# Linear attention feeding a GELU MLP on one core: block-diagonal states from chunk 4 on, outputs beside the next scores, and an opening with more idle matmuls

## The chip, the cores and the metric

The kernel runs on one core of a Trainium2 chip. The metric is the device time of one execution in microseconds (us). Before the change the median of eight runs is 226.21 us, with 225.3 the fastest and 226.98 the slowest. One execution was also taken with the hardware profiler: it took 225.3 us, and the span of its instructions is 223.3 us, so that 2.0 us lie around the span.

## What is computed

Two stages follow each other. The first is decayed linear attention over blocks, for 4 sequences of 768 positions, 8 heads and 64 channels a head. The second is an MLP with exact GELU over the 3072 tokens, 512 to 2048 to 512.

```
for b in range(nb):                      # block = 64
    intra = (q_b @ k_b.T * Dmask) @ v_b
    inter = (q_b * lam_pow) @ kv_state
    out_b = intra + inter
    kv_state = lam**block * kv_state + (k_b * rev_pow).T @ v_b
...
x = out.transpose(0, 2, 1, 3).reshape(B * S, H * D)
h = x @ w_in
out = gelu(h) @ w_out
```

## The kernel before

The kernel takes the sequence in chunks of 128 positions, six to a sequence and 24 in all. Four chunks make a group of 512 tokens, and there are six groups. While TensorE does the MLP of group g, it also does the attention of the four chunks that make group g+1, in short stretches between the MLP's blocks of four matmuls. The opening does chunks 0 to 3 by themselves, with nothing to put beside them but idle matmuls on zeros (L321) that keep TensorE busy. The MLP of the last group has no attention beside it.

A chunk has these steps. `load` brings k, q and v by DMAs that POOL issues. `decay_k` scales k by a power of the decay. The transposes of k and q come either from TensorE (`transposes`, chunks 0 to 7) or from SP's transposing DMAs (`dma_transposes`, chunks 8 to 23), the latter after POOL has scaled q to `q_hat`. `scores` makes eight products, each with 64 rows of the array (L189), and VectorE (DVE) masks them (L193). `next_state` makes the new state: eight products with 64 columns of the array (L202), then DVE adds the decayed old state, and POOL (or ACT in the opening) decays the sum for the next chunk (L212, L214). `outputs` adds eight products of 64 rows by 64 columns with the state (L223) and eight with 64 columns for the masked scores (L227), and the result is cast into `x_t` (by ACT in the opening, L231, by DVE later, L233).

The MLP of a group is 16 blocks `mm1` (L245, four matmuls of 512 columns, then a GELU on ACT) and 16 blocks `mm2` (L257, likewise four, and a copy and a store after every fourth block of an output row).

What sets the order: every engine runs its instructions in program order. For groups 1 to 5 the list `todo` gives each chunk's steps a place as a fraction of the group's MLP, and the loop at the end puts a step before the first block that is not earlier than its place. Scores with the new state stand at one place and the outputs of the same chunk about half a chunk later, so each chunk breaks into the MLP twice. Loads are issued by `prefetch`, called at the step `begin`. PSUM has eight banks: two each for the tags `sc`, `mh` and `mo`, one each for `o` and `t`. The pool `work` has three buffers for each tag, so `k_dec` of a chunk can be written once the state product of the chunk three before it has read its own.

Of the kernel before, what the change touches and what calls it, by code (L numbers as in the profile page):

```python
# [8 lines left out]
F32 = mybir.dt.float32  # L9
BF16 = mybir.dt.bfloat16  # L10
# [5 lines left out]
def kernel(  # L16
# [24 lines left out]
    NG = NCH // M  # L41
    assert NG * M == NCH

# [103 lines left out]
    def decay_k(c, eng):  # L147

        if c.sb == NB - 1:
            return  # L150
        c.k_dec = work_pool.tile([128, H, D], BF16, tag="kd", name="k_dec")
        if eng is nc.scalar:
            for h in range(H):
                nc.scalar.activation(c.k_dec[:, h, :], c.k[:, h, :], ACT.Copy, scale=lam_k[:, h:h + 1])
        else:
            eng.tensor_mul(c.k_dec, c.k, lam_k[:, :, None].to_broadcast((128, H, D)))  # L156

    def transposes(c):
        if c.early:

            t_ps = [bank([128, HP, C], BF16, tag, "t_ps") for tag in ("mh", "mo")]
        else:
# [6 lines left out]
        c.qT = work_pool.tile([128, HP, C], BF16, tag="qT", name="qT")  # L169
        if c.early and c.n > 0:  # L170
            nc.scalar.copy(c.kT, t_ps[0])
        else:
            nc.vector.tensor_copy(c.kT, t_ps[0])  # L173
# [21 lines left out]
    def next_state(c):  # L195
        if c.sb == NB - 1:
            return
        kv_ps = bank([128, HP, D], F32, "t", "kv_ps")
        for hp in range(HP):
            for hi in range(2):  # L200
                h = 2 * hp + hi
                nc.tensor.matmul(kv_ps[hi * D:(hi + 1) * D, hp, :], c.k_dec[:, h, :], c.v[:, h, :],  # L202
                                 start=True, stop=True)
        new = work_pool.tile([128, HP, D], BF16, tag="state", name="state")
        if c.sb == 0:
# [3 lines left out]
        old = work_pool.tile([128, HP, D], F32, tag="old", name="old")  # L209
        if c.early:  # L210
            for hp in range(HP):
                nc.scalar.activation(old[:, hp, :], new[:, hp, :], ACT.Copy, scale=lam_c[:, hp:hp + 1])  # L212
        elif c.sb < NB - 2:
            nc.gpsimd.tensor_mul(old, new, lam_c_b)  # L214
        states[c.n + 1] = new, old

    def outputs(c, x_t, off):
        o_ps = bank([128, HP, C], F32, "o", "o_ps")
        if c.sb > 0:
            for hp in range(HP):  # L220
# [8 lines left out]
        x_o = x_t[:, :, off * C:(off + 1) * C]  # L229
        if c.early:  # L230
            nc.scalar.copy(x_o, o_ps)  # L231
        else:
            nc.vector.tensor_copy(x_o, o_ps)  # L233
# [75 lines left out]
    nc.scalar.activation(warm, pos, ACT.Gelu)  # L309

    def early(s):
# [4 lines left out]
    idle_ps = bank([128, 512], F32, "o", "idle_ps")  # L316

    def keep_warm(n):

        for _ in range(n):  # L320
            nc.tensor.matmul(idle_ps, idle[:, :128], idle, start=True, stop=True)  # L321

# [6 lines left out]
    keep_warm(2)  # L329
    next_state(live[0])  # L330
    outputs(live[0], xT[0], 0)
# [12 lines left out]
    for s in range(1, NS):  # L344
# [3 lines left out]


    total = NK2 * 4 * M * C + M * NK2 * 512  # L350
    todo = []
    for n in range(M, NCH):
        g, i = n // M - 1, n % M
        first, end = (0.66, 1.0) if g == 0 else (0.0, 0.97)
        at = lambda f: (g + first + (end - first) * (i + f) / M) * total
# [4 lines left out]
    def step(kind, n):  # L360
        g = n // M - 1
        if kind == 0:
            live[n] = begin(n)
            if g > 0:
                dma_transposes(live[n])
            decay_k(live[n], nc.gpsimd)
            prefetch(n + 4)
        elif kind == 1:
            if g == 0:
                transposes(live[n])  # L370
        elif kind == 2:
# [4 lines left out]

    prefetch(2 * M - 1)
    done = 0
    for g in range(NG):
        if g + 1 < NG:  # L380
            alloc_x(g + 1)
        for run, cost in mlp_blocks(g):
            while todo and todo[0][0] <= done:
# [36 lines left out]
```

## Time and profile before

| what | value |
|---|---|
| median of eight runs | 226.21 us (225.3 to 226.98) |
| profiled execution, its span | 225.3 us, 223.3 us |
| TensorE matmul busy | 213.7 us of the span |
| DVE, ACT, POOL busy | 61.4, 89.2, 111.6 us |
| chain that ended last | 78% TensorE |

The eight runs are 225.3, 226.67, 226.98, 225.91, 226.5, 226.78, 225.4 and 225.73 us. The profile's page gives each engine's busy time and the chain of work that ended last. Its views go further: the timeline lists the instructions in order of time with the idle time before each and what ended it, and the view by stretches sums the busy time of each engine between two times and gives the clock that TensorE was granted there, 1.00 being full. A matmul's own duration includes its way through the array, so the pace of a run of matmuls is read from one start to the next.

### The profile page before, as it was taken

To read this page: it belongs to the slowest core of one execution; us is meant where nothing else is said; L and a number is where in the kernel's file an instruction comes from. 1 tells how busy PE (TensorE), PEld (TensorE's weight loads), DVE (VectorE), ACT (ScalarE), POOL (GpSimd) and SP (SyncE) were. 2 spreads that over 40 slices of the span, in tenths; PEclk is the share of its full clock that TensorE was granted. 3 is DMA by queue.
4 is the path that set the end of the run, shared out by engine and by line. 5 is a ranking of instruction groups with operands and counts; after the bars stand their busy time and mean duration, and the time that the engine had idled before them with its cause. 6 is when DMAs were issued, how large, how long until landed. Compare 5 with 4: busy or idle time off the path is not lost.

```text
span 223.3 us, 3859 instructions
## 1 busy us (share of the span) xinstructions
PE 213.7 (96%) x1571; PEld 102.2 (46%) x1571; DVE 61.4 (27%) x109; ACT 89.2 (40%) x173; POOL 111.6 (50%) x132
## 2 busy tenths in 40 slices
PE   7886999899899999999999999999999999999993
PEld 2354444455444444444444444444444444444452
DVE  3575000267542142142142142142142142100000
ACT  6895665110356412255312356311346311467121
POOL 8998333899999994054855991043141000000000
PEclk9995899999999999999999999999999999999998
DMA  6999999999999999759679999013331111200112
GB/s 41 144 162 183 195 206 182 154 205 151 146 153 155 148 127 148 138 90 112 55 89 131 175 149 158 1 50 103 109 74 23 23 50 68 74 0 3 47 47 94
DMA packets 100273, 24.37 MB, mean 109 GB/s; under 512 B 92960, under 2 KB 97312, under 8 KB 100256
## 3 DMA queue, kind: packets, MB, share of 16 engines
q0 software_dynamic: 79104, 13.64, 85.3%
q1 hardware_dynamic: 21152, 10.50, 21.5%
q8 instruction: 12, 0.20, 0.4%
q14 instruction: 5, 0.04, 0.1%
HBM read 27.27 MB, written 6.29 MB: 150 GB/s over the span
## 4 chain that ended last, share of the span: by engine, by line
PE 78%; DMA 10%; POOL 9%; issue 1%; DVE 0%; ACT 0%; POOLq 0%
PE o_ps L257 34%; PE h_ps L245 32%; DMA w_out_t<-in_moe_w_out_dram 8%; PE o_ps L227 3%; PE sc_ps L189 3%; PE o_ps L223 3%; DMA k_t<-in_k_dram 2%; POOL q_t L65 2%; POOL v_t L65 2%; PE kv_ps L202 2%; POOL k_t L65 2%; PE o_ps L272 2%; POOL w_in_t L87 1%; POOL w_out_t L91 1%; POOL k_dec L156 1%
## 5 line engine op out<-in xcount | busy, mean ns | idle before, releaser
L245 PE MATMUL h_ps<-x_t,w_in_t 128*128 128x512 bf16 x384 | 87.6, 383 | 1.2 <-DVE x_t L233 0.8
L257 PE MATMUL o_ps<-w_out_t,g_t 128*128 128x512 bf16 x368 | 84.6, 380 | 0.0
L247 ACT ACTIVATE g_t<-h_ps 128x512 bf16<-128x512 f32 x96 | 57.3, 597 | 38.9 <-PE h_ps L245 38.9
L245 PEld LDWEIGHTS <-w_in_t 128*128 128x128 bf16 x384 | 36.5, 98 | 44.3 <-issue 2.6
L257 PEld LDWEIGHTS <-g_t 128*128 128x128 bf16 x368 | 34.0, 98 | 39.5
L193 DVE TENSOR_TENSOR sc_m<-sc_ps,dmask 128x512 bf16<-128x512 f32 x48 | 30.9, 686 | 65.7 <-PE sc_ps L189 65.5
L262 ACT COPY o_sb<-o_ps 128x512 f32<-128x512 f32 x23 | 13.5, 586 | 84.3 <-PE o_ps L257 81.0
L214 POOL TENSOR_TENSOR old<-state,lam_c 128x256 f32<-128x256 bf16 x12 | 7.4, 618 | 48.4 <-DVE state L208 25.1
L65 POOL DMA_DIRECT2D k_t<-in_k_dram x24 | 22.1, 922 | 3.7 <-DMA w_out_t<-in_moe_w_out_dram 1.7
L65 POOL DMA_DIRECT2D q_t<-in_q_dram x24 | 21.5, 895 | 4.9 <-DMA w_out_t<-in_moe_w_out_dram 3.3
L233 DVE CAST x_t<-o_ps 128x512 bf16<-128x512 f32 x20 | 13.8, 690 | 35.6 <-PE o_ps L227 35.6
L65 POOL DMA_DIRECT2D v_t<-in_v_dram x24 | 21.3, 889 | 3.9 <-DMA w_in_t<-in_moe_w_in_dram 1.7
L156 POOL TENSOR_TENSOR k_dec<-k_t,lam_k 128x512 bf16<-128x512 bf16 x18 | 19.0, 1053 | 0.5 <-DMA k_t<-in_k_dram 0.4
L181 POOL TENSOR_TENSOR q_hat<-q_t,lam_p 128x512 bf16<-128x512 bf16 x16 | 16.8, 1047 | 0.0
L227 PE MATMUL o_ps<-sc_m,v_t 128*64 128x128 bf16 x192 | 10.6, 232 | 0.0
L189 PEld LDWEIGHTS <-kT 64*128 64x128 bf16 x192 | 5.7, 97 | 9.9 <-issue 8.0
L189 PE MATMUL sc_ps<-qT,kT 64*128 64x128 bf16 x192 | 10.0, 226 | 0.2 <-DVE qT L174 0.2
L223 PE MATMUL o_ps<-qT,state 64*64 64x128 bf16 x160 | 8.7, 230 | 1.3 <-ACT x_t L231 1.3
L223 PEld LDWEIGHTS <-state 64*64 64x64 bf16 x160 | 5.5, 110 | 8.1 <-issue 7.8
L321 PE MATMUL idle_ps<-idle 128*128 128x512 bf16 x19 | 8.0, 579 | 1.2 <-DVE idle L94 1.2
L173 DVE COPY kT<-t_ps 128x512 bf16<-128x512 bf16 x5 | 2.1, 422 | 22.3 <-PE t_ps L167 22.2
L227 PEld LDWEIGHTS <-v_t 128*64 128x64 bf16 x192 | 6.4, 113 | 3.1 <-issue 1.4
(42 smaller groups left out, 75.4 us busy)
## 6 DMA issues: line engine op xcount, KB each, us to landing
out_dram<-o_sb SPq DMA_DIRECT2D x23, 256.0 KB, 2.5
k_t<-in_k_dram POOLq DMA_DIRECT2D x24, 128.0 KB, 5.0
q_t<-in_q_dram POOLq DMA_DIRECT2D x24, 128.0 KB, 5.2
v_t<-in_v_dram POOLq DMA_DIRECT2D x24, 128.0 KB, 5.8
w_in_t<-in_moe_w_in_dram POOLq DMA_DIRECT2D x4, 512.0 KB, 8.7
w_out_t<-in_moe_w_out_dram POOLq DMA_DIRECT2D x4, 512.0 KB, 15.5
kT<-k_t SPq DMA_TRANSPOSE x16, 4.9
qT<-q_hat SPq DMA_TRANSPOSE x16, 4.1
```

Of the source, the lines that this page charges most:

```text
L65: nc.gpsimd.dma_start(raw[n, name], chunk_of(name, n))
L156: eng.tensor_mul(c.k_dec, c.k, lam_k[:, :, None].to_broadcast((128, H, D)))
L181: nc.gpsimd.tensor_mul(q_hat, c.q, lam_p[:, :, None].to_broadcast((128, H, D)))
L189: nc.tensor.matmul(sc_ps[hi][:, hp, :], c.kT[p, hp, :], c.qT[p, hp, :], start=True, stop=True)
L193: nc.vector.tensor_mul(c.sc_m[:, :, hi, :], sc_ps[hi], dmask_r[:, :, hi, :])
L223: nc.tensor.matmul(o_ps[p, hp, :], states[c.n][0][p, hp, :], c.qT[p, hp, :], start=(hp == 0), stop=False, skip_group_check=True)
L227: nc.tensor.matmul(o_ps[hi * D:(hi + 1) * D, hp, :], c.v[:, 2 * hp + hi, :], c.sc_m[:, hp, hi, :], start=(c.sb == 0 and hp == 0), stop=Tru ...
L233: nc.vector.tensor_copy(x_o, o_ps)
L245: nc.tensor.matmul(h_ps, w_in_t[:, ki, kf * 128:(kf + 1) * 128], x_t[:, ki, :], start=(ki == 0), stop=(ki == NK1 - 1))
L247: nc.scalar.activation(g_t[:, kf, :], h_ps, ACT.Gelu)
L257: nc.tensor.matmul(om[io], g_t[:, kf, io * C:(io + 1) * C], w_out_t[:, kf, :], start=(kf == 0), stop=(kf == NK2 - 1))
L262: nc.scalar.copy(o_sb, om[io])
```

## The change

From chunk 4 on, the state is kept as a full 128 by 128 block for each pair of heads, with zeros off the diagonal blocks: four products of 128x128 make it, and four products use it, in place of eight and eight on parts of the array. The new DVE steps multiply by `lam_blk`, which holds the decay on the diagonal blocks and zero elsewhere; the decay on POOL is gone. Chunk 3 writes its state into the zeroed `first_blk`. The scale of k from chunk 4 on is `lam_m`. In groups 1 to 5 the outputs of a chunk are put at the same place as the scores of the next. Beside group 0's MLP the steps of chunks 4 to 7 stand in a table written by hand, `group0`, by the number of the block. POOL's loads and scalings for chunks 4 to 9 are written out. In the opening the decay of k for chunk 1 moves from ACT to DVE, chunk 2's scores move ahead of chunk 1's outputs, chunk 3's state product moves into group 0's MLP, and nine idle matmuls are added (28 against 19).

```diff
+    lam_blk = consts.tile([128, HP, 128], F32)
+    first_blk = consts.tile([128, HP, 128], BF16)
+    nc.vector.memset(lam_blk, 0.0)
+    nc.vector.memset(first_blk, 0.0)
...
+    def make_lam_blk():
+        for hi in range(2):
+            p = slice(hi * D, (hi + 1) * D)
+            nc.vector.tensor_copy(lam_blk[p, :, p], lam_c_b[p])
...
-            eng.tensor_mul(c.k_dec, c.k, lam_k[:, :, None].to_broadcast((128, H, D)))
+            scale = lam_k if c.early else lam_m
+            eng.tensor_mul(c.k_dec, c.k, scale[:, :, None].to_broadcast((128, H, D)))
...
-            both = bank([128, 2, HP, C], BF16, "t", "t_ps")
-            t_ps = [both[:, 0], both[:, 1]]
+        t_ps = [bank([128, HP, C], BF16, tag, "t_ps") for tag in ("mh", "mo" if c.early else "mh")]
...
-        if c.early and c.n > 0:
+        if c.n > 0:
             nc.scalar.copy(c.kT, t_ps[0])
...
+        if not c.early:
+            return next_state_full(c)
...
+        if c.n == M - 1:
+            for hi in range(2):
+                p = slice(hi * D, (hi + 1) * D)
+                nc.vector.tensor_add(first_blk[p, :, p], kv_ps[p], states[c.n][1][p])
+            states[c.n + 1] = first_blk, None
+            return
...
+    def next_state_full(c):
+
+        kv_ps = bank([128, HP, 128], F32, "t", "kv_ps")
+        for hp in range(HP):
+            nc.tensor.matmul(kv_ps[:, hp, :], c.k_dec[:, 2 * hp:2 * hp + 2, :], c.v[:, 2 * hp:2 * hp + 2, :],
+                             start=True, stop=True)
+        new = work_pool.tile([128, HP, 128], BF16, tag="state_f", name="state")
+        if c.sb == 0:
+            nc.vector.tensor_mul(new, kv_ps, lam_blk)
+        else:
+            tmp = work_pool.tile([128, HP, 128], F32, tag="tmp", name="tmp")
+            nc.vector.tensor_add(tmp, kv_ps, states[c.n][0])
+            nc.vector.tensor_mul(new, tmp, lam_blk)
+        states[c.n + 1] = new, None
+
+    def outputs(c, x_t, off):
+        o_ps = bank([128, HP, C], F32, "mh" if c.n == M - 1 else "o", "o_ps")
+        if c.sb > 0 and not c.early:
             for hp in range(HP):
...
-        elif c.sb < NB - 2:
-            nc.gpsimd.tensor_mul(old, new, lam_c_b)
...
+                nc.tensor.matmul(o_ps[:, hp, :], states[c.n][0][:, hp, :], c.qT[:, hp, :],
+                                 start=(hp == 0), stop=False, skip_group_check=True)
...
-        if c.early:
+        if c.n < 2 * M:
             nc.scalar.copy(x_o, o_ps)
...
+        if s == 1:
+            decay_k(live[s], nc.vector)
         transposes(live[s])
-        decay_k(live[s], nc.scalar if s < 2 else nc.gpsimd)
...
+    keep_warm(1)
     early(2)
     next_state(live[1])
+    scores(live[2])
+    decay_state(live[1])
+    outputs(live[1], xT[0], 1)
+    keep_warm(1)
     early(3)
-    outputs(live[1], xT[0], 1)
-    scores(live[2])
     next_state(live[2])
     outputs(live[2], xT[0], 2)
     scores(live[3])
+    keep_warm(5)
     outputs(live[3], xT[0], 3)
-    next_state(live[3])
+    decay_state(live[2])
+    make_lam_blk()
+    keep_warm(2)
...
+    for n, name in [(4, "k"), (4, "q"), (4, "v"), (5, "k"), (5, "q"), (5, "v"), (6, "k"), (6, "q")]:
+        load(n, name)
+    begin_decayed(4)
+    for n, name in [(6, "v"), (7, "k"), (7, "q"), (7, "v"), (8, "k")]:
+        load(n, name)
+    live[5] = begin(5)
+    begin_decayed(6)
+    for n, name in [(8, "q"), (8, "v")]:
+        load(n, name)
+    begin_decayed(7)
+    next_load[0] = 9
+    prefetch(9)
...
+    group0 = {
+        1: [lambda: next_state(live[3])],
+        22: [lambda: transposes(live[4])],
+        24: [lambda: scores(live[4])],
+        25: [lambda: transposes(live[5]), lambda: next_state(live[4]), lambda: x1(4)],
+        26: [lambda: scores(live[5])],
+        27: [lambda: transposes(live[6])],
+        28: [lambda: x1(5), lambda: scores(live[6])],
+        29: [lambda: transposes(live[7]), lambda: next_state(live[6])],
+        30: [lambda: x1(6), lambda: scores(live[7])],
+        31: [lambda: next_state(live[7]), lambda: x1(7)],
+    }
...
-        fs = (-0.5, 0.0, 0.5, 1.05) if g == 0 else (-0.45 if n == 2 * M else -1.0, 0.0, 0.35, 0.75)
-        todo += [(at(f), kind, n) for kind, f in enumerate(fs)]
+        at = 0.06 + 0.245 * i
+        fs = [at - (0.18 if n == 2 * M else 0.32), None, at, at + 0.245 if i < M - 1 else 0.965]
+        todo += [(round((g + f) * total), -kind, n) for kind, f in enumerate(fs) if f is not None]
...
-            prefetch(n + 4)
+            prefetch(n + 3)
```

TensorE, end of the opening: what follows chunk 3's scores (`sc_ps`). Before, the products with the state and with the masked scores, then chunk 3's own state product (`kv_ps`), then the MLP (`h_ps`):

```order
L189 MATMUL sc_ps_379<-qT,kT 128x128
...
L223 MATMUL o_ps<-qT,state 64x128
...
L227 MATMUL o_ps<-sc_m,v_t 64x128
...
L202 MATMUL kv_ps<-v_t,k_dec 64x64
...
L245 MATMUL h_ps<-x_t,w_in_t 128x512
```

The same place now:

```order
L196 MATMUL sc_ps_379<-qT,kT 128x128
...
L349 MATMUL idle_ps<-idle 128x512
...
L257 MATMUL o_ps<-qT,state 64x128
...
L261 MATMUL o_ps<-sc_m,v_t 64x128
...
L349 MATMUL idle_ps<-idle 128x512
...
L279 MATMUL h_ps<-x_t,w_in_t 128x512
...
L211 MATMUL kv_ps<-v_t,k_dec 64x64
```

Five idle matmuls stand between scores and outputs and two behind the outputs, and the state product has moved behind the MLP's first block.

TensorE, group 1, one chunk's part of the MLP before: scores and state product (`kv_ps`) at one place, the state's and scores' outputs at another, 12 MLP matmuls between them:

```order
L245 MATMUL h_ps<-x_t,w_in_t 128x512
...
L189 MATMUL sc_ps_1024<-qT,kT 128x128
...
L202 MATMUL kv_ps<-v_t,k_dec 64x64
...
L245 MATMUL h_ps<-x_t,w_in_t 128x512
...
L223 MATMUL o_ps<-qT,state 64x128
...
L227 MATMUL o_ps<-sc_m,v_t 64x128
...
L245 MATMUL h_ps<-x_t,w_in_t 128x512
```

And now, where chunk 8's outputs and chunk 9's scores meet:

```order
L279 MATMUL h_ps<-x_t,w_in_t 128x512
...
L251 MATMUL o_ps<-qT,state 128x128
...
L261 MATMUL o_ps<-sc_m,v_t 64x128
...
L196 MATMUL sc_ps_993<-qT,kT 128x128
...
L236 MATMUL kv_ps<-v_t,k_dec 128x128
...
L279 MATMUL h_ps<-x_t,w_in_t 128x512
```

One stretch has taken the place of two; the products with full 128x128 blocks (L251 and L236, four each) stand at its two ends.

POOL, from the loads of chunk 6 to the scaling of chunk 8's q. Before, the scaling of chunk 4's k (`k_dec`) came after chunk 7's loads; one piece of the difference:

```order
 L65 DMA q_t<-in_q_dram 128x8x64 [waits DMASW3_49]
-L65 DMA v_t<-in_v_dram 128x8x64 [waits DMASW4_49]
+L167 TENSOR_TENSOR k_dec<-k_t,lam_m 128x512 [waits DMASW4_49,DVE_49,PE_49]
+L65 DMA v_t<-in_v_dram 128x8x64
 L65 DMA k_t<-in_k_dram 128x8x64 [waits DMASW5_49]
 L65 DMA q_t<-in_q_dram 128x8x64 [waits DMASW6_49]
 L65 DMA v_t<-in_v_dram 128x8x64 [waits DMASW7_49]
-L156 TENSOR_TENSOR k_dec<-k_t,lam_k 128x512 [waits PE_49,Activation_49]
 L65 DMA k_t<-in_k_dram 128x8x64 [waits DMASW0_49]
+L167 TENSOR_TENSOR k_dec<-k_t,lam_m 128x512 [waits DMASW2_49,PE_49,Pool_49]
+L65 DMA q_t<-in_q_dram 128x8x64 [waits DMASW1_49]
```

The scalings of chunks 4 and 6 have moved ahead among the loads, and chunk 8's `q_hat` is the seventh instruction behind chunk 6's scaling: behind chunk 9's loads and ahead of chunk 10's.

More of the change, by code (lines that the diff above doesn't have):

```diff
@@ L41 @@
     NG = NCH // M
-    assert NG * M == NCH
+    assert NG * M == NCH and M == 4 and NB == 6
     ctx.enter_context(tc.manual_schedule())
@@ L309, with keep_warm @@
     nc.scalar.activation(warm, pos, ACT.Gelu)
+    def keep_warm(n):
+        idle_ps = bank([128, 512], F32, "mo", "idle_ps")
+        for _ in range(n):
+            nc.tensor.matmul(idle_ps, idle[:, :128], idle, start=True, stop=True)
     def early(s):
         live[s] = begin(s, early=True)
+        if s == 1:
+            decay_k(live[s], nc.vector)
         transposes(live[s])
-        decay_k(live[s], nc.scalar if s < 2 else nc.gpsimd)
[L316 to L321, printed above, removed]
+        if s != 1:
+            decay_k(live[s], nc.scalar if s == 0 else nc.gpsimd)
     keep_warm(9)
@@ L330 @@
     next_state(live[0])
+    decay_state(live[0])
     outputs(live[0], xT[0], 0)
@@ L381 @@
             alloc_x(g + 1)
-        for run, cost in mlp_blocks(g):
+        for i, (run, cost) in enumerate(mlp_blocks(g)):
+            if g == 0:
+                for act in group0.get(i, []):
+                    act()
             while todo and todo[0][0] <= done:
```

33 lines of the change are left out of this document (14 added, 19 removed).

## The prediction

> **What bounds the kernel now.** I read the page first, for the whole span.
>
> ```profile
> span 223.3 us, 3859 instructions
> PEclk9995899999999999999999999999999999999998
> PE 78%; DMA 10%; POOL 9%; issue 1%; DVE 0%; ACT 0%; POOLq 0%
> ```
>
> TensorE is most of the chain that ended last; the DMA and POOL shares lie in the opening. The granted clock falls in the fourth and fifth of 40 slices. So I cut the span into the opening, group 0 (first MLP matmul to group 1's first) and the rest; two answers of the view by stretches:
>
> ```profile
> 17.10:20.55 3.45, 2.57 (x33) 1.78 (x33) 2.27 (x5) 1.89 (x6) 3.45 (x6) 0.51 1.16 170
> 20.55:23.96 3.41, 2.93 (x21) 1.48 (x20) 0.45 (x2) 1.82 (x6) 1.79 (x3) 0.50 1.24 206
> 23.96:37.00 13.04, 13.04 (x62) 5.96 (x61) 0.00 (x0) 8.88 (x16) 4.38 (x5) 1.00 1.29 199
> ```
>
> ```profile
> 21.89:59.41 37.52, 36.05 (x273) 17.58 (x273) 12.77 (x24) 12.97 (x24) 25.69 (x29) 0.97 1.97 180
> 59.41:92.68 33.27, 33.27 (x249) 15.38 (x249) 8.91 (x15) 11.31 (x19) 26.93 (x31) 1.00 1.84 148
> ```
>
> Group 1 is TensorE from end to end (33.27 of 33.27 us). From 17.1 to 23.96 the clock is half. What one chunk costs TensorE is read from starts in the timeline, beside the pace of undisturbed MLP matmuls in the chain (13.81/64 = 0.216 us each):
>
> ```profile
> 192.21 13.81 PE h_ps L245 x64
> ```
>
> ```profile
> 59.41 2.75 PE L245 MATMUL h_ps<-x_t,w_in_t 128*128 128x512 bf16 x12 [0.79 <-DVE x_t L233]
> 62.09 0.40 PE L189 MATMUL sc_ps<-qT,kT 64*128 64x128 bf16 x8
> 62.41 0.32 PE L202 MATMUL kv_ps<-v_t,k_dec 128*64 128x64 bf16 x8
> 62.66 2.76 PE L245 MATMUL h_ps<-x_t,w_in_t 128*128 128x512 bf16 x12
> 65.36 0.41 PE L223 MATMUL o_ps<-qT,state 64*64 64x128 bf16 x8
> 65.70 0.41 PE L227 MATMUL o_ps<-sc_m,v_t 128*64 128x128 bf16 x8
> 66.05 4.49 PE L245 MATMUL h_ps<-x_t,w_in_t 128*128 128x512 bf16 x20
> ...
> 52.73 1.90 PE L257 MATMUL o_ps<-w_out_t,g_t 128*128 128x512 bf16 x8
> 54.47 0.39 PE L167 MATMUL t_ps<-ident,k_t 128*128 128x128 bf16 x4
> 54.69 0.39 PE L167 MATMUL t_ps<-ident,q_t 128*128 128x128 bf16 x4
> 55.01 0.41 PE L227 MATMUL o_ps<-sc_m,v_t 128*64 128x128 bf16 x8
> ```
>
> Twelve MLP matmuls should take 2.59; they take 2.68 before scores and 2.70 before outputs. Transposes, which use the whole array, start 1.74 after eight MLP matmuls, as 8 x 0.216 asks, and four of them take 0.22 (0.055 each); from the last four to the half-array product it is 0.32. So a **turn** from whole-array products to a part costs about 0.10. I take the same 0.10 for a turn between two kinds of parts, and for one back to the whole, where it sits inside the 0.32, 0.25, 0.34 and 0.35 us of the four sets above.
>
> The Trainium skill has a rule for it ("TensorEngine Tiling (Array Packing)", Key Properties): changing the tiling mode drains the engine. The rows agree, at 0.10 us.
>
> **Groups 1 to 5, part by part.** A chunk costs now 0.09 + 0.32 + 0.25 + 0.01 = 0.68 at its first place and 0.11 + 0.34 + 0.35 = 0.79 at its second: 1.47, with six turns. After: four whole-array state products 4 x 0.055 = 0.22 with no turn, a turn 0.10, eight products 0.35, eight scores 0.33, four whole-array products for the new state 0.22, no turn: 1.22, with three turns. That is 0.25 less for a chunk whose outputs meet the next scores. The new products do not occur in the trace; the transposes are the nearest row (0.055). I take it. The other end is twice the parts' time without their turn, 0.48 and 0.30, which makes the chunk 1.56 and the change a loss of 0.09 a chunk (third rival); faster than the transposes they can't be by much, since those wait for nothing.
>
> The first chunk of a group has its scores alone (0.65 for 0.68) and the last its outputs alone (0.67 for 0.79); sequence starts lack the state's output, sequence ends the new state. By group I get 5.64 to 4.75, 5.55 to 4.74, 5.30 to 4.53 and 5.64 to 4.75: **-3.4**. The check: 33.27 - 128 x 0.216 = 5.65 for group 1. DVE gets two steps of 512 elements in place of one of 256, 6 us ahead of their use; at ACT and POOL nothing waits. At a group's end one block (0.86) is left between the last outputs and group 1's kind of start, where the cast with its latencies needs 0.87: hidden to the hundredth, up to 0.1 each if not.
>
> By the same page's Theoretical Speedup a contraction of 64 runs up to twice as fast in parts, so whole products full of zeros would be a loss; that is the third rival.
>
> **Group 0.** It takes 37.52, of which 27.6 are MLP matmuls; the clock at half until 23.96 costs (23.96 - 21.89)/2 = 1.03, and TensorE waits three times:
>
> ```profile
> 43.61 0.40 PE L189 MATMUL sc_ps<-qT,kT 64*128 64x128 bf16 x8 [0.25 <-DVE qT L174]
> 44.45 0.32 PE L202 MATMUL kv_ps<-v_t,k_dec 128*64 128x64 bf16 x8 [0.44 <-POOL k_dec L156]
> ```
>
> with the 0.79 above at group 1's start. Now the attention there is, block by block of the table: chunk 3's state 0.35; four transposes of eight 4 x 0.44; scores of 4 and 5 alone 0.43 each; chunk 4's state and outputs 0.90; chunk 5's outputs with scores 6 1.00; state 6 0.22; outputs 6 with scores 7 0.78; state and outputs of 7 0.90. Sum 6.8; with 27.6, 34.4: **-3.1** if the clock is full and nothing waits. I followed DVE through it (q 0.69, masks 1.29, state 2 x 0.69 a chunk, rows below; the multiply with both inputs in SBUF by half of L128's 1.22): the last masks end about when chunk 7's outputs want them; that multiply at 1.22 would still end in time, since chunk 5's outputs come 2 us after it.
>
> **The opening.** Rows of the timeline, for durations and for what the end waits for:
>
> ```profile
> 5.17 1.22 DVE L128 TENSOR_TENSOR dmask<-cmask,lam_m 128x1024 f32<-128x1024 f32 x1 [0.79 <-ACT lam_m L119]
> ...
> 13.54 1.05 ACT L212 ACTIVATE old<-state,lam_c 128x64 f32<-128x64 bf16 x4
> 14.49 0.57 ACT L231 CAST x_t<-o_ps 128x512 bf16<-128x512 f32 x1
> 14.63 0.42 DVE L208 TENSOR_TENSOR state<-kv_ps,old 128x256 bf16<-128x256 f32 x1
> 14.96 0.58 ACT L171 COPY kT<-t_ps 128x512 bf16<-128x512 bf16 x1
> 15.05 0.40 PE L167 MATMUL t_ps<-ident,q_t 128*128 128x128 bf16 x4 [0.42 <-DMA q_t<-in_q_dram]
> 15.48 0.69 DVE L174 TENSOR_TENSOR qT<-t_ps,lam_q 128x512 bf16<-128x512 bf16 x1 [0.43 <-PE t_ps L167]
> 16.49 1.29 DVE L193 TENSOR_TENSOR sc_m<-sc_ps,dmask 128x512 bf16<-128x512 f32 x2 [0.32 <-PE sc_ps L189]
> 19.73 0.64 PE L223 MATMUL o_ps<-qT,state 64*64 64x128 bf16 x8 [0.47 <-ACT x_t L231]
> 20.52 0.94 POOL L65 DMA_DIRECT2D k_t<-in_k_dram  x1
> 21.89 14.98 PE L245 MATMUL h_ps<-x_t,w_in_t 128*128 128x512 bf16 x64 [0.46 <-ACT x_t L231]
> ```
>
> After, ACT has no 2 us of scaling for chunk 1 (DVE does it in 0.69, POOL's 1.05 at most, ahead of a step that has that slack), but chunk 2's scores now wait for ACT: decay until 13.6, cast 14.0, copy of k 14.6. From there: scores 2 at 14.7, outputs 1 15.0, one idle 15.7, transposes 3 16.0, state 2 16.5, outputs 2 16.75 to 17.45, scores 3 to 17.8, their masks 1.29 to 19.3 with five idle matmuls beside them, outputs 3 to 19.75, cast 0.57 from 19.95, MLP at **20.6**: -1.3. It can't be before about 20.5: chunk 4's k load, issued at 20.52 without a wait, waits for the same semaphore as the first weights. At half clock from 17.1, as now, the idle matmuls cost 5 x 0.43 and the MLP starts at about 21.9. The two memsets lie in DVE's wait for ACT's first results, at most 0.6 each by L128; gone, they would delay the decay tables by that.
>
> **Transposes of chunks 8 and 9.** Group 1 comes 4.4 earlier, so scores 8 are wanted at 56.9 and scores 9 at 65.0.
>
> ```profile
> 38.32 0.88 POOL L65 DMA_DIRECT2D q_t<-in_q_dram  x1 [1.66 <-DMA w_out_t<-in_moe_w_out_dram]
> 43.34 1.05 POOL L156 TENSOR_TENSOR k_dec<-k_t,lam_k 128x512 bf16<-128x512 bf16 x1
> 58.65 1.19 SPq L182 DMA_TRANSPOSE qT<-q_hat  x1
> ```
>
> ```profile
> DMA to landing us min/median/max: 2.4/4.1/5.9
> ```
>
> POOL is at chunk 6's q at 38.3 as now. Behind it stand ten loads (0.9) and three scalings (1.05) before `q_hat` 8: 52 to 53, and its transpose lands after 2.4 to 5.9: 55.5 to 59, median 57.2. Chunk 9's `q_hat` follows one scaling and six loads later, about 60.8, lands 63 to 66.7, median 65. Waits of **+0.6** in all, 0 to 2. Later chunks gain: POOL has 4.8 of work for about 8 us of TensorE.
>
> **Sum, against the profiled execution.** -3.4 - 3.1 - 1.3 + 0.6 = -7.2: 225.3 - 7.2 = 218.1, span 216.1. The median of the eight runs lies 0.9 above that execution; half of it I keep, since a clock that recovers before the MLP leaves less to chance: **218.6**, likeliest 217.2 to 219.8.
>
> The Trainium skill ("TensorE: Matmul & The Clock Gate", Part 1) says that activity is judged in free-running windows of about 3.4 us and a busy one frees the clock. By it a run loses 0 to 1.7 at the MLP's start before, which is the eight runs' spread of 1.7, and with the new idle matmuls little: 217.8. The trace's half-clock stretch of 6.9 us agrees with two windows.
>
> **Rivals.**
> - The idle matmuls don't hold the clock (for it: at 2.57 of 3.45 us busy the present opening did not get it back). No gain from 20.6, nor the 1.03, and no waits: -5.4 from the profiled run, 219.9, and 220.8 with the median's whole 0.9.
> - Transposes land late, 2.0 instead of 0.6: 220.0. For it, 5.9 of the slowest landing; against, fewer transposes in flight then.
> - The whole-array products bring nothing, so groups 1 to 5 keep their time, 222.0, or lose 16 x 0.09 besides, 223.4. Against it, 0.055 a transpose and no turn before it.
> - Slower than before: POOL stands at one of the scalings moved ahead of the loads, and every load, `q_hat` and score behind it slips.
>
> ```profile
> POOL old L214 <- DVE state L206: 23.3, 2, 12.1
> ```
>
> POOL has stood 12.1 for DVE at a time. Such a wait ahead of `q_hat` 8 gives 218.6 + 11.5 = 230.1; it decides from about 8 us on. Against it: the scalings wait only for products three chunks back, done in the opening or by 44.
>
> **How the numbers follow.** Forecast 0.55, clock lost 0.18, late transposes 0.16, no gain in whole products 0.07, POOL stands 0.04. The range is 217.0 (no waits, MLP at 20.5, and turns of 0.11, of which 48 go) to 221.2; it holds most of the first three, and leaves out the last two and the tails. Within 0.3% is what a measurement can't tell from no change; 0.01 of the third rival with waits falls there. Faster 0.95, same 0.01, slower 0.04.
>
> **What would show it.** Group 1 to 4 stretches of 32.4 instead of 33.2, whole-array products starting 0.055 apart with no 0.10 ahead; the clock 1.00 at the first MLP matmul, near 20.6; group 0 at 34.4; a wait of TensorE for chunk 8's or 9's transposes below 1 us. Half clock at the MLP's start, whole products 0.1 apart, or a wait of several us for `qT` would make it wrong.

## The result and the profile after

| | before | after |
|---|---|---|
| median of the runs compared | 226.29 us (32 runs, 225.07 to 227.78) | 218.27 us (11 runs, 217.74 to 220.83) |
| profiled execution, its span | 225.3 us, 223.3 us | 218.72 us, 216.9 us |

The medians lie 8.0 us apart. The ratio is 0.9667, with a 95% interval of 0.964 to 0.9693; it is taken over all the runs compared and not from the medians, and by it the change is worth 7.5 us. In what follows, medians and ratios leave out the executions that took over 1.5% longer than the fastest of their kernel: one of e5 (274.24 us), two of e6 (221.93 and 222.23), three of e8 (224.05 to 224.65) and one of e11 (220.34). The page of the changed kernel, the granted clock in 40 slices and the chain of work that ended last:

```profile
PEclk9999999999999999999999999999999999999999
PE 75%; DMA 16%; POOL 6%; issue 1%; ACT 0%; POOLq 0%
```

The dip of the clock in the fourth and fifth slices is gone. But the DMA share of the chain has grown from 10% to 16%. The view by stretches, for the second of the two windows that the prediction showed at half clock, then group 0 (first MLP matmul to group 1's first) and groups 1 to 4; each row has PE, PEld, DVE, ACT and POOL busy, the clock, the DMA share and GB/s:

```profile
20.55:23.96 3.41, 3.41 (x24) 1.49 (x22) 0.84 (x2) 1.79 (x3) 1.79 (x3) 1.00 1.24 206
19.98:55.85 35.87, 34.80 (x256) 17.36 (x257) 12.06 (x19) 16.29 (x29) 22.89 (x26) 1.00 1.69 177
55.85:88.65 32.80, 32.48 (x221) 15.96 (x220) 11.91 (x19) 11.90 (x20) 31.48 (x34) 1.00 2.08 160
88.65:121.07 32.42, 32.42 (x222) 15.83 (x220) 12.60 (x19) 11.90 (x20) 19.43 (x21) 1.00 1.30 128
121.07:153.26 32.19, 32.19 (x217) 15.61 (x216) 10.81 (x17) 11.90 (x20) 12.92 (x14) 1.00 0.69 90
153.26:185.68 32.42, 32.42 (x222) 15.92 (x220) 11.50 (x18) 11.90 (x20) 0.00 (x0) 1.00 0.22 58
```

The clock is 1.00 where it was 0.50. Group 0 holds 1.07 us in which TensorE is idle (35.87 - 34.80), group 1 holds 0.32, groups 2 to 4 nothing. (In the runs below, idle time of 0.16 to 0.42 in such a row can be one or two matmuls whose records are missing; the waits named are those of the timeline.) The timeline of TensorE names what it waited for:

```profile
19.98 1.04 PE L279 MATMUL h_ps<-x_t,w_in_t 128*128 128x512 bf16 x4 [0.76 <-DMA w_in_t<-in_moe_w_in_dram]
21.20 13.12 PE L279 MATMUL h_ps<-x_t,w_in_t 128*128 128x512 bf16 x60
...
40.00 0.40 PE L174 MATMUL t_ps<-ident,k_t 128*128 128x128 bf16 x4 [0.50 <-DMA k_t<-in_k_dram]
40.97 0.40 PE L174 MATMUL t_ps<-ident,q_t 128*128 128x128 bf16 x4 [0.57 <-DMA q_t<-in_q_dram]
...
58.05 0.40 PE L196 MATMUL sc_ps<-qT,kT 64*128 64x128 bf16 x8 [0.32 <-DMA qT<-q_hat]
```

Every wait from 19.98 on is for a DMA: the first weights, chunk 4's k and q, chunk 8's transposed q. The end of the opening on ACT and TensorE, to be read against the prediction's steps:

```profile
13.71 0.40 PE L196 MATMUL sc_ps<-qT,kT 64*128 64x128 bf16 x8 [0.64 <-ACT kT L178]
...
18.73 0.59 ACT L265 CAST x_t<-o_ps 128x512 bf16<-128x512 f32 x1 [1.61 <-PE o_ps L261]
```

The last cast ends at 19.32 (18.73 + 0.59), 0.66 before the first MLP matmul, which then waits for weights alone. The chain, in order of time, has the load behind the second of those waits:

```profile
22.75 18.17 DMA q_t<-in_q_dram
```

Chunk 4's q, issued at 22.75, takes 18.17 us to land, behind the weights. And where chunk 8's outputs meet chunk 9's scores, TensorE's timeline reads:

```profile
63.80 1.89 PE L279 MATMUL h_ps<-x_t,w_in_t 128*128 128x512 bf16 x8
65.53 0.39 PE L251 MATMUL o_ps<-qT,state 128*128 128x128 bf16 x4
65.84 0.41 PE L261 MATMUL o_ps<-sc_m,v_t 128*64 128x128 bf16 x8
66.19 0.40 PE L196 MATMUL sc_ps<-qT,kT 64*128 64x128 bf16 x8
66.52 0.40 PE L236 MATMUL kv_ps<-v_t,k_dec 128*128 128x128 bf16 x4
66.76 1.46 PE L279 MATMUL h_ps<-x_t,w_in_t 128*128 128x512 bf16 x6
```

Eight MLP matmuls start 1.73 apart from the first state product, as 8 x 0.216 asks, so there is no turn ahead of it. From the first state product to the next MLP matmul it is 66.76 - 65.53 = 1.23; the prediction had 1.22. The four whole-array products of the new state take 0.24 of it (66.52 to 66.76), where the eight on parts took 0.25 in the kernel before (62.41 to 62.66).

### The profile page after: what moved, and what is told of

Its sections match the earlier page's. It is cut to its first block, busy times and chain, and to the rows that moved or that the text cites. A ratio compares the mean times of both kernels' runs of the same rounds, so it can differ in the third digit from the quotient of the medians.

```text
span 216.9 us, 3573 instructions
## 1 busy us (share of the span) xinstructions
PE 207.8 (96%) x1448; PEld 102.6 (47%) x1448; DVE 72.7 (33%) x120; ACT 91.0 (42%) x169; POOL 105.4 (49%) x120
## 4 chain that ended last, share of the span: by engine, by line
PE 75%; DMA 16%; POOL 6%; issue 1%; ACT 0%; POOLq 0%
PE o_ps L291 33%; PE h_ps L279 31%; DMA q_t<-in_q_dram 8%; DMA w_in_t<-in_moe_w_in_dram 3%; PE sc_ps L196 3%; PE o_ps L261 3%; DMA k_t<-in_k_dram 2%; PE kv_ps L236 2%; DMA qT<-q_hat 2%; POOL k_t L65 2%; POOL q_t L65 2%; PE o_ps L306 2%; POOL v_t L65 2%; PE o_ps L251 2%; POOL k_dec L167 1%
## 5 line engine op out<-in xcount | busy, mean ns | idle before, releaser
L279 PE MATMUL h_ps<-x_t,w_in_t 128*128 128x512 bf16 x384 | 85.4, 379 | 0.8 <-DMA w_in_t<-in_moe_w_in_dram 0.8
L291 PEld LDWEIGHTS <-g_t 128*128 128x128 bf16 x368 | 34.6, 98 | 39.7
L267 DVE CAST x_t<-o_ps 128x512 bf16<-128x512 f32 x16 | 11.1, 692 | 73.0 <-PE o_ps L261 73.0
L188 POOL TENSOR_TENSOR q_hat<-q_t,lam_p 128x512 bf16<-128x512 bf16 x16 | 16.9, 1056 | 17.5 <-DMA qT<-q_hat 17.1
L167 POOL TENSOR_TENSOR k_dec<-k_t,lam_m 128x512 bf16<-128x512 bf16 x16 | 17.2, 1078 | 14.7 <-PE kv_ps L236 8.7
L181 DVE TENSOR_TENSOR qT<-t_ps,lam_q 128x512 bf16<-128x512 bf16 x8 | 5.5, 689 | 20.3 <-PE t_ps L174 20.0
L349 PE MATMUL idle_ps<-idle 128*128 128x512 bf16 x28 | 9.3, 462 | 1.2 <-DVE idle L94 1.2
L244 DVE TENSOR_TENSOR state<-tmp,lam_blk 128x512 bf16<-128x512 f32 x13 | 10.2, 781 | 0.4
L261 PE MATMUL o_ps<-sc_m,v_t 128*64 128x128 bf16 x192 | 9.9, 225 | 0.0
L178 ACT COPY kT<-t_ps 128x512 bf16<-128x512 bf16 x7 | 4.1, 581 | 9.8 <-PE t_ps L174 9.8
L243 DVE TENSOR_TENSOR tmp<-kv_ps,state 128x512 f32<-128x512 f32 x12 | 8.2, 680 | 0.0
```

The costliest lines, as they stand in the source:

```text
L167: eng.tensor_mul(c.k_dec, c.k, scale[:, :, None].to_broadcast((128, H, D)))
L188: nc.gpsimd.tensor_mul(q_hat, c.q, lam_p[:, :, None].to_broadcast((128, H, D)))
L244: nc.vector.tensor_mul(new, tmp, lam_blk)
L261: nc.tensor.matmul(o_ps[hi * D:(hi + 1) * D, hp, :], c.v[:, 2 * hp + hi, :], c.sc_m[:, hp, hi, :], start=(c.sb == 0 and hp == 0), stop=Tru ...
L279: nc.tensor.matmul(h_ps, w_in_t[:, ki, kf * 128:(kf + 1) * 128], x_t[:, ki, :], start=(ki == 0), stop=(ki == NK1 - 1))
L291: nc.tensor.matmul(om[io], g_t[:, kf, io * C:(io + 1) * C], w_out_t[:, kf, :], start=(kf == 0), stop=(kf == NK2 - 1))
```

## The experiments

The main theory: each turn between whole-array products and a part of the array costs 0.10 us; the changed groups have fewer turns and products that cost no more; and what stops the rest of the gain is loads that land late. Rivals: whole-array products are the gain and turns cost nothing, or the nine added idle matmuls (the clock) are the gain. All times are medians; the ratio in brackets is to the kernel before, with its 95% interval.

**e1: the state's products behind the masked scores' products.** The same products, with more turns.

```diff
 outputs(c, x_t, off)
-    four products with the state, then eight with the masked scores
+    eight products with the masked scores, then four with the state
```

> The changed kernel with the same products in another order: from chunk 4 on the four whole-array state products of an output come behind the eight products of the masked scores instead of ahead of them. Theory of turns (each change between whole-array products and a part of the array costs about 0.10 us): eleven stretches have four turns instead of three, ten in groups 1 to 4 and one in group 0, so +1.1 us, about 219.4. Rival (the gain lies in the products themselves, fewer and larger): the same products, no change, 218.3.

Measured 219.84 us (0.9718, 0.968 to 0.9757). The median is near the turn theory's, but it is not the proof, since this run's trace differs in its loads too: group 1 starts at 54.56 (55.85 in the changed kernel), and chunk 9's scores then wait 1.15 us for `qT`. Groups 2, 3 and 4 have no such wait and decide it. Their rows by stretches:

```profile
88.61:121.31 32.70, 32.49 (x217) 15.54 (x220) 12.60 (x19) 11.90 (x20) 18.58 (x20) 1.00 1.19 118
121.31:153.80 32.49, 32.28 (x214) 15.35 (x216) 10.82 (x17) 11.90 (x20) 12.73 (x14) 1.00 0.68 90
153.80:186.62 32.82, 32.50 (x218) 15.58 (x221) 11.51 (x18) 11.90 (x20) 0.00 (x0) 1.00 0.21 57
```

They are 0.28, 0.30 and 0.40 longer than in the changed kernel, 0.98 together. Where it lies is read from TensorE's timeline at the end of group 3 and at one chunk of group 4; first the changed kernel, then e1 (in which one record of the 32 MLP matmuls is missing):

```profile
152.39 1.04 PE L291 MATMUL o_ps<-w_out_t,g_t 128*128 128x512 bf16 x4
153.26 1.03 PE L279 MATMUL h_ps<-x_t,w_in_t 128*128 128x512 bf16 x4
...
155.65 7.07 PE L279 MATMUL h_ps<-x_t,w_in_t 128*128 128x512 bf16 x32
162.56 0.39 PE L251 MATMUL o_ps<-qT,state 128*128 128x128 bf16 x4
...
163.78 0.59 PE L279 MATMUL h_ps<-x_t,w_in_t 128*128 128x512 bf16 x2
```

```profile
152.85 1.03 PE L292 MATMUL o_ps<-w_out_t,g_t 128*128 128x512 bf16 x4
153.80 1.46 PE L280 MATMUL h_ps<-x_t,w_in_t 128*128 128x512 bf16 x6
...
156.18 7.07 PE L280 MATMUL h_ps<-x_t,w_in_t 128*128 128x512 bf16 x31
163.18 0.41 PE L258 MATMUL o_ps<-sc_m,v_t 128*64 128x128 bf16 x8
...
164.42 0.81 PE L280 MATMUL h_ps<-x_t,w_in_t 128*128 128x512 bf16 x2
```

From one MLP stretch to the next the chunk takes 8.24 in e1 (156.18 to 164.42) and 8.13 in the changed kernel: 0.11 for its one added turn. It stands where the theory has it, ahead of the masked products: the MLP's 32 matmuls take 7.00 to them, and 6.91 to the whole-array state products of the changed kernel. Groups 2, 3 and 4 have two, two and three such chunks, 0.77 of the 0.98. The rest is at the groups' ends, where the whole-array products come last and the next group's first matmul waits for the cast, which ends at 153.74 in e1: 0.95 from the last MLP block's start in e1, 0.87 in the changed kernel, 0.08 at each of three ends (group 3's is shown). That is the cover which the prediction called hidden to the hundredth.

**e2 and e3: the two parts of groups 1 to 5 apart.** e2 has whole-array products, with scores and outputs at the two places of before. e3 has the products on parts of the array, at the new places.

```diff
 e2:
-        at = 0.06 + 0.245 * i
-        fs = [at - (0.18 if n == 2 * M else 0.32), None, at, at + 0.245 if i < M - 1 else 0.965]
+        at = lambda f: (g + 0.97 * (i + f) / M) * total
+        fs = [-0.45 if n == 2 * M else -1.0, None, 0.35, 0.75]
 e3:
-        if not c.early:
-            return next_state_full(c)
-        if c.sb > 0 and not c.early:
+        if False:
```

> The changed kernel, but in groups 1 to 5 the outputs stand again at a place of their own, half a chunk behind the scores, as before; products are whole-array as changed. Theory of turns: twelve stretches are cut in two, each with one turn more and its 0.01 of restart, +1.3 us, about 219.6. Rival (places do nothing): 218.3.

> The changed kernel with the states in parts as before (eight products each, k scaled as before; the old state is decayed on VectorE), in the new order. Theory of turns: groups 1 to 4 save 0.105 at each of 12 meetings only, so they are 1.9 us slower than changed, and group 0 some 0.7 with its parts: about 220.9. Rival (the new places and table carry all of the gain): 218.3.

Measured 219.88 (0.9715, 0.9689 to 0.974) and 221.14 (0.9772, 0.9745 to 0.9799), both within 0.3 of what was expected. The medians alone prove little, since other things moved too: in the profiled executions chunk 9's scores waited 0.96 us for `qT` in e2 and 1.81 in e3, and neither waited for chunk 4's loads. Group 2, behind all that, decides. It is shown by stretches in the kernel before, in e2 and in e3, a fence for each:

```profile
92.68:125.85 33.17, 33.17 (x250) 15.33 (x248) 9.24 (x16) 11.90 (x20) 20.16 (x24) 1.00 0.91 102
```

```profile
20.50:54.93 34.43, 34.06 (x251) 17.41 (x256) 11.86 (x19) 16.91 (x31) 22.15 (x26) 1.00 1.76 182
88.70:121.43 32.73, 32.31 (x217) 15.61 (x220) 13.23 (x19) 11.90 (x20) 19.66 (x21) 1.00 1.24 126
```

```profile
90.30:123.15 32.85, 32.43 (x245) 15.55 (x248) 11.35 (x20) 11.90 (x20) 20.99 (x24) 1.00 1.07 113
```

Whole products alone take 0.44 off group 2, the places alone 0.32. Together that is 0.76, and both at once took 33.17 to 32.42: 0.75. The two parts add, and neither is empty. The 0.32 is three meetings of 0.10. The 0.44 is nearly all at the state's outputs, of which group 2 has three: with no turn ahead of them they take 0.31 (65.53 to 65.84 above) where the kernel before had a turn of 0.11 and 0.34, so 0.14 less each. The new state's products gain 0.01. The first row of e2 is its group 0, which waited for no load: 34.43, where 34.4 was predicted.

**e4: without the nine added idle matmuls.**

```diff
     load_w_in(0)
-    keep_warm(1)
...
     outputs(live[1], xT[0], 1)
-    keep_warm(1)
...
-    keep_warm(5)
     outputs(live[3], xT[0], 3)
...
     make_lam_blk()
-    keep_warm(2)
```

> The changed kernel without the nine added idle matmuls. Theory that loads cap the opening: chunk 4's transposes, which waited 1.07 us for k and q in the profile, wait for less, and the time stays within 0.5 us, 218.3 to 218.8. Rival (the idle matmuls hold the clock and carry the opening's gain): half clock at the MLP's start again, +1 to +2 us, 219.3 to 220.3.

Measured 218.9 (0.9681, 0.965 to 0.9713). The median is 0.1 above the loads theory's range and 0.4 below the rival's. Its stretches: the one at half clock and group 0.

```profile
20.64:24.05 3.41, 3.41 (x16) 1.18 (x16) 0.84 (x2) 1.32 (x4) 0.94 (x2) 0.50 1.24 206
20.11:56.12 36.01, 35.64 (x251) 17.82 (x256) 11.86 (x19) 16.91 (x31) 23.20 (x27) 0.95 1.74 179
```

This run lost 3.41 / 2 = 1.7 us to the clock and its span is 216.9 all the same. Group 0, 0.14 longer than in the changed kernel, has no wait for chunk 4's loads, and group 1, 32.42, none for `qT`. In these two executions time won in the opening is waited away again for loads. By the medians the nine idle matmuls are worth 0.6 us; the two intervals overlap, so that is not settled.

**e5: the opening and group 0 of before, with the changed groups 1 to 5.**

```diff
-    (the new opening, group0's table and the loads written out)
+    (the opening of before, group 0's places in todo, prefetch(n + 4))
```

> The changed groups 1 to 5 (whole-array states, outputs beside the next scores) behind the opening of before, and group 0 placed as before with its loads as before, though with whole-array states. Theory: groups 1 to 5 bring their 3.1 us and group 0's whole-array products 0.3 to 0.7, so 222.5 to 223.0; the other 4 to 5 us lie in the opening's and group 0's order. Rival (the opening changes little because loads cap it): under 220.

Measured 224.58 (0.9909, 0.9875 to 0.9942), 1.6 above what was expected: a miss. The eleven runs compared fall into two sets, four from 222.58 to 222.83 and seven from 224.41 to 225.72. The profiled one is of the first set, 222.77, as expected. Its stretches, the one at half clock, group 0, and group 2:

```profile
16.24:26.48 10.24, 8.85 (x70) 4.64 (x70) 4.33 (x9) 3.62 (x9) 6.88 (x9) 0.50 1.21 191
21.39:60.13 38.74, 36.39 (x244) 17.98 (x249) 15.92 (x29) 11.89 (x20) 26.52 (x29) 0.93 1.92 179
92.70:125.12 32.42, 32.21 (x218) 15.84 (x221) 12.66 (x19) 11.89 (x20) 20.97 (x23) 1.00 1.09 114
```

Group 2 has the changed pace, 32.42, behind the old opening: that part stands by itself. What made the second set 2 us slower was not traced. In five of its seven runs the mean clock was 0.968 to 0.970, against 0.974 to 0.977 in the first set, which is about 1.7 us more lost to half clock; the other two, at 0.977 and 0.985, it does not explain, and they stay open.

**e6 to e8: earlier loads and later use.** If late loads are the cap, moving them should gain. e6 asks for chunk 4's transposes one block later. e7 loads chunk 8's q ahead of chunk 7's v and scales it ahead of chunk 9's loads. e8 does both.

```diff
 e6, e8:
-        22: [lambda: transposes(live[4])],
+        23: [lambda: transposes(live[4])],
 e7, e8:
-    for n, name in [(6, "v"), (7, "k"), (7, "q"), (7, "v"), (8, "k")]:
+    for n, name in [(6, "v"), (7, "k"), (7, "q"), (8, "k"), (8, "q"), (7, "v")]:
...
+    q_hat8 = work_pool.tile([128, H, D], BF16, tag="qh", name="q_hat")
+    nc.gpsimd.tensor_mul(q_hat8, raw[8, "q"], lam_p[:, :, None].to_broadcast((128, H, D)))
     next_load[0] = 9
     prefetch(9)
```

> The changed kernel with chunk 4's transposes one MLP block later (23 in place of 22), where k and q have landed. Theory that two loads cap it one after the other: the wait of 1.07 us goes, but the wait for chunk 8's transposed q grows by as much, since its load hangs on the loads queue and not on TensorE: 218.1 to 218.4. Rival (the first wait alone counts): 217.4.

> The changed kernel with chunk 8's k and q loaded ahead of chunk 7's v, and its q scaled before chunk 9's loads: about 2 us earlier. Theory: the wait of 0.32 us before chunk 8's scores goes, and no more: 218.0. Rival (chunk 7's later v delays its products): 218.3 or above.

> Both edits together. Theory of two caps in a row: now the first wait's 0.9 us and the second's 0.32 both come out, 217.1 to 217.4. Rival (another wait behind them, on VectorE's or ACT's chain in group 0, takes their place): 218.0.

Measured 218.59 (0.9655, 0.9616 to 0.9694), 222.3 (0.9822, 0.9784 to 0.9859) and, over three runs from 220.12 to 223.37, 223.32 (0.9826, 0.9762 to 0.989). The first is 0.2 above what was expected; the last two are clear misses, 4.3 and 5.9 us above. The waits view of e6 from 40 to 75 us (us in total, times, longest):

```profile
PE sc_ps L196 <- DMA qT<-q_hat: 2.1, 2, 1.5
```

What e6 won in group 0 (34.45, no wait) came back as waits for `qT`. Its edit need not be what won it: chunk 4's k and q landed at about 38.8 and 39.8 in this run, 1.1 earlier than in the changed kernel, and at the old block they would have been wanted at about 39.5 and 39.8. In e7 the wait sits at chunk 9's scores, by TensorE's timeline, 3.51 us; e8's is 4.21. What led to it stands in e7's timeline of POOL:

```profile
68.33 0.40 PE L199 MATMUL sc_ps<-qT,kT 64*128 64x128 bf16 x8 [3.51 <-DMA qT<-q_hat]
```

```profile
54.98 0.92 POOL L65 DMA_DIRECT2D k_t<-in_k_dram  x1
...
59.37 0.91 POOL L65 DMA_DIRECT2D v_t<-in_v_dram  x1
60.27 1.09 POOL L191 TENSOR_TENSOR q_hat<-q_t,lam_p 128x512 bf16<-128x512 bf16 x1
```

Chunk 9's scaling of q stands behind six loads (chunks 10 and 11), 54.98 to 60.27, and its transpose, issued at 61.38, lands only at about 68.2. The changed kernel has the same six loads ahead of the scaling; it starts at 59.76 there, the transpose lands at about 65.8, and chunk 9's scores at 66.19 do not wait. So about 1.4 of the 3.5 us come from TensorE being at these scores earlier (64.75 for 66.19), 0.5 from POOL and 1.8 from a longer landing (6.8 us from issue to landing, for 5.0), less the 0.35 that the changed kernel had to spare. New theory: those six loads, on POOL and in the DMA engines, are what chunk 9 hangs on.

The wait costs more than its length. The clock of e8 in 40 slices:

```profile
PEclk9999999999998899999999999999999999999999
```

It falls in the 13th and 14th slice: from 69.70 to 73.10, right behind the wait that ends at 69.12, its mean is 0.51, and 1.7 us are lost besides. In e7 four of the six executions have a mean clock of 0.992, some 3.5 us at half clock, and took 222.2 to 223.38; the two at 1.00, of which the profiled one is the faster, took 220.86 and 221.51. Where the half clock lay in those four was not traced.

**e9 to e11: three of the six loads moved behind chunk 9's scaling.** e9 is the changed kernel with that edit, e10 is e7 with it, e11 is e8 with it.

```diff
-            prefetch(n + 3)
+            prefetch(n + 3 if n > 2 * M else n + 2)
```

> The changed kernel, but with the loads of chunk 10 alone behind chunk 8's steps on POOL, and chunk 11's and 12's behind chunk 9's: three loads (2.6 us) move from ahead of chunk 9's scaled q to behind it. In the changed kernel chunk 9's transposed q lands 0.35 us before it is wanted, so TensorE has no wait there to lose: 218.3 (217.9 to 218.7), with chunk 9's transpose landing at about 62 to 63 us in place of 65.84. If those six loads were needed so early, chunks 10 and 11 would be late and it would be above 219.

> Chunk 8's q loaded earlier, as in the run of that name that took 222.3 us, and three loads moved behind chunk 9's scaled q. If that run lost its 3.5 us because chunk 9's scaled q and its transpose stood behind the six loads of chunks 10 and 11, the wait goes and the gain of the earlier transpose of chunk 8 shows: 217.9 (217.6 to 218.4), with waits for qT below 0.3 us. If the loss is of another kind, it stays at or above 221.

> The same with chunk 4's transposes one block of the MLP later, so that they don't wait for chunk 4's k and q (1.07 us in the changed kernel). If loads that land late are all that is left, both gains show: 217.1 (216.7 to 217.6). If group 1 then comes too early for chunk 8's or 9's transposes, a wait for qT takes the gain back: 218 to 219.5. If the loss of the run with both edits (223.71) was of another kind, above 221.

Measured 218.21 (0.9657, 0.9632 to 0.9681), 218.13 (0.9661, 0.9631 to 0.9692) and 217.51 (0.9637, 0.9607 to 0.9667). The one line takes 4.2 us off e7 and 5.8 off e8, half clock included. Chunk 9's scaling and scores in e10's timeline, of POOL and of TensorE:

```profile
58.98 1.06 POOL L191 TENSOR_TENSOR q_hat<-q_t,lam_p 128x512 bf16<-128x512 bf16 x1
```

```profile
65.41 0.40 PE L199 MATMUL sc_ps<-qT,kT 64*128 64x128 bf16 x8
```

The scaling starts 1.3 earlier than in e7, with three loads before it, and chunk 9's scores follow at 65.41 with no wait shown. So the theory holds for the loads' place on POOL; from e8 to e11 the scaling starts 2.5 earlier, 58.70 for 61.25. For the loads in the DMA engines it is not shown: e11's transpose took 6.5 us to land and e8's 6.6, and over all traces it was 5.2 to 6.5 behind three loads (e9 to e12) and 5.0 to 7.6 behind six (the changed kernel, e1 to e3 and e6 to e8). In e9 the landing came 2.0 us earlier, not the 2.8 to 3.8 that were expected, and the time stayed, since nothing waited there. e11 has the lowest median of all. Its interval overlaps with that of the changed kernel (0.964 to 0.9693), so that it beats it is likely and not settled; its profiled execution, of 220.34 us, waited 2.38 us for the first weights and then had 3.4 us at half clock, with all 28 idle matmuls in place.

**e12: chunk 4's k and q loaded ahead of `w_out`, on top of e10.**

```diff
     for s in range(1, NS):
         load_w_in(s)
+    load(4, "k")
+    load(4, "q")
     for s in range(NS):
         load_w_out(s)
```

> The run with chunk 8's q loaded earlier and three loads moved (218.13), and besides chunk 4's k and q loaded ahead of the four loads of w_out. If what caps group 0 is how much the DMA engines have moved by then, not the order of the loads, the last quarter of w_out, wanted in the block behind chunk 4's transposes, lands some 1.9 us later (two loads that land 0.9 apart), and TensorE waits about 1 us for it in place of chunk 4's k and q: 218.1 (217.7 to 218.5). If only the place of those two loads in the order was the cap, the wait of 0.6 to 1.1 goes and none comes: 217.3 (216.9 to 217.6).

Measured 217.97 (0.9639, 0.9596 to 0.9683), as the first theory had it, but not by its step. TensorE's timeline:

```profile
39.19 0.39 PE L174 MATMUL t_ps<-ident,q_t 128*128 128x128 bf16 x4
39.62 1.89 PE L294 MATMUL o_ps<-w_out_t,g_t 128*128 128x512 bf16 x8
...
56.74 0.40 PE L199 MATMUL sc_ps<-qT,kT 64*128 64x128 bf16 x8 [0.59 <-DMA qT<-q_hat]
```

The wait for chunk 4's loads is gone. The next MLP block starts 0.43 behind the transposes of q, about 0.2 more than those take, not 1 us. Group 1 starts at 54.26, and then `qT` is late twice, 0.59 at chunk 8 and 1.08 at chunk 9. Both theories were half right: the order was the cap at chunk 4, and the time comes back at the next transfer that is late.

## Why the prediction was right, and where it was off

By the forecast's own terms, from one profiled execution to the other:

| term | predicted | measured |
|---|---|---|
| opening, to the first MLP matmul | -1.3 (20.6) | -1.9 (19.98) |
| group 0 | -3.1 (34.4) | -1.65 (35.87) |
| groups 1 to 5 | -3.4 | -3.1 |
| waits for transposes of chunks 8 and 9 | +0.6 | +0.3 |
| sum | -7.2 | -6.4 |

The measured third term is 59.41 to 192.05 before, 132.64, against 55.85 to 185.69 after, 129.84, less the wait of 0.32. The last group did not change.

**Groups 1 to 5: right, by the mechanism named.** The state products start with no turn ahead of them, a chunk takes 1.23 for 1.22, and e1 prices the turn at 0.11 for 0.10. The term was sized 0.3 too large: group 2, for one, lost 0.75 where 5.55 - 4.74 = 0.81 was worked out. The third rival, whole products full of zeros as no gain, falls by e2: whole products alone take 0.44 off group 2. Nearly all of that is the turn saved ahead of the state's outputs.

**The opening: the right direction, two steps mis-sized.** Chunk 2's scores came at 13.71, not 14.7, and the last cast at 18.73, not 19.95. The floor of 20.5 was wrong: that chunk 4's k load did not wait at 20.52 shows that the first weights had landed by then, not that they landed then. In the changed kernel that load starts at 20.52 again, and the weights, issued at 11.98, let the MLP start at 19.98. The clock held in the profiled execution, as forecast; e4 shows that without the nine matmuls it need not, and e11 that with them it need not either. The first rival priced a clock that does not hold at 219.9 to 220.8; e4 had half clock at the MLP's start and took 218.9; the loss took the place of waits for loads.

**Group 0: the step that failed is "if nothing waits".** The work was sized well: e2 did it in 34.43 without a wait for loads, and in the changed kernel chunk 3's state, for one, takes 0.36 (21.20 - 19.98, less 0.86 for four MLP matmuls) where 0.35 was priced. Nearly all of the miss of 1.5 lies at chunk 4's transposes. The 24 MLP matmuls from 34.16 on have k's due at 39.34, and they start at 40.00; q's are due 0.22 behind k's and start 0.97 behind. That is 0.66 and 0.75 from start to start, 1.41 in all; the 1.07 of idle time is less, because the matmuls before are counted as busy up to their ends.

The prediction looked for waits at chunk 8's transposes alone. The trace before had what was needed: there chunk 4's k and q, issued at 20.52 and 23.01, land 18.4 and 16.9 us later, at about 38.9 and 39.9, and the prediction's own schedule wants them at about 40.0 and 40.2. That left q a margin of 0.3, and more than that was lost: TensorE came 0.6 earlier than forecast, and the loads landed some 1.0 later than before, at about 39.9 and 40.9. In the traces of the runs up to e10 they land between 38.4 and 39.9 and between 39.3 and 40.9; why the changed kernel's profiled execution has the latest is open. That they land late because they stand behind the weights is shown by e12: ahead of `w_out`, they took 10.3 us. The table has the exchange: 0.6 more won in the opening, 1.4 less in group 0.

**Transposes of chunks 8 and 9: right, for the changed kernel.** Chunk 8's scores waited 0.32, chunk 9's not at all. But the margin is thin: e1 waited 1.15 and e12 1.08 at chunk 9, where group 1 began some 1.3 to 1.6 earlier, and e2 0.96 and e3 1.81.

**The median.** The sum was 0.8 too hopeful for the span; the profiled execution, 218.72 for 218.1, only 0.6, since 1.8 us lie around its span and not 2.0. The median was 0.3 too high all the same, because I kept 0.45 between profiled execution and median, and the changed kernel's median lies 0.45 below its profiled execution. Part of the nearness to 218.27 is thus luck, two errors against each other. The lower end of the range does not follow from its terms either: 0.6, 0.1 and 0.48 below 218.6 are 217.4, and 217.0 is what they leave of 218.1. The result lies inside either way.

The Trainium skill ("TensorE: Matmul & The Clock Gate", Part 1) has activity judged in windows of about 3.4 us. The stretches at half clock agree: 3.41 in e4 and 10.24, three times that, in e5. Ahead of such a stretch TensorE had been busy for 1.86 of 3.41 us in e4 (17.23 to 20.64) and for 2.27 of 3.40 in the kernel before (13.70 to 17.10); in the changed kernel it was 2.69 of 3.45 from 17.10 to 20.55, and the clock stayed at 1.00. Where the line lies, no run here shows.

## What to carry to other kernels

Read the price of a turn between array shapes from starts in the timeline, count turns, and put products of one shape next to each other; at 0.10 us a turn, four products full of zeros on half their blocks came out cheaper than eight exact ones at the outputs, where they saved the turn ahead (0.31 us for 0.45), and about as dear for the new state (0.24 for 0.25). When an early stage is made faster, list the landing time of each transfer behind it, from the trace before, and set it against the new schedule before adding up the gain: in e6, e7 and e12 one wait was gone, and the time was paid at the next. Loads issued between one chunk's preparation and the next one's stand in the way of the latter: moving three of them was worth 4 to 6 us in e10 and e11, where TensorE waited for the latter, and nothing in e9, where it did not.

## What was not expected of the hardware

The multiply with both inputs in SBUF (L244) took 0.69 us ten times out of 13, and 1.02 to 1.19 three times; the add before it, with one input in PSUM (L243), never left 0.68. The timeline of the changed kernel, DVE beside POOL, at two of the three:

```profile
60.39 1.02 DVE L244 TENSOR_TENSOR state<-tmp,lam_blk 128x512 bf16<-128x512 f32 x1
60.77 1.54 POOL L167 TENSOR_TENSOR k_dec<-k_t,lam_m 128x512 bf16<-128x512 bf16 x1
...
101.08 1.19 DVE L244 TENSOR_TENSOR state<-tmp,lam_blk 128x512 bf16<-128x512 f32 x1
101.16 0.90 POOL L65 DMA_DIRECT2D q_t<-in_q_dram  x1
```

At 60.39 POOL's scaling runs beside it and is itself longer, 1.54 against some 1.05. The Trainium skill ("SBUF — State Buffer", Who interferes with whom) says that a DVE instruction with two SBUF inputs contends with a GpSimd instruction that reads SBUF, and one with a single SBUF input does not. The rows at 60.39 and L243's even 0.68 agree. At 101.08 there is only the issue of loads on POOL, which the rule does not account for, and what stretched it there is open. Nothing waited for these multiplies, so it cost no time.

The other surprise is how much the landing of one transposing DMA differs between nearly equal kernels. Chunk 9's `qT` took 5.0 us from issue to landing in the changed kernel and 6.8 in e7, with the same six loads ahead of it on POOL, and 7.6 in e3. What sets it is open.
